# Routing's subtractions, products and constants from VectorE to GpSimd, with new offsets for the planner

## The chip, the cores and the metric

The kernel runs on one core of a Trainium2 chip. Its engines are TensorE (PE; PEld is its weight load), VectorE (DVE), ScalarE (ACT), GpSimd (POOL) and SyncE (SP, which here issues most of the DMAs). The metric is the time of one execution on the device, in microseconds (us), as the median of some runs. Engine times and the granted TensorE clock come from the profile of one execution.

## The reference

Attention in which each query keeps its 32 largest scores, then a mixture of eight experts, each token going to one expert or, by a skip gate, to none. Cut to what matters:

```python
B, H, S, D = 8, 8, 576, 64
scores = scale * np.matmul(q, k.transpose(0, 1, 3, 2))
kth = np.partition(scores, -32, axis=-1)[..., -32:-31]
scores = np.where(scores >= kth, scores, -1e9)
attn = softmax(scores)                      # with 1e-9 in the denominator
x = (attn @ v) as (B*S, H*D)                # N = 4608 tokens, DM = 512
do_compute = x @ w_skip > 0
e_idx = argmax(x @ w_gate, axis=1)          # E = 8 experts
gate_w = softmax(x @ w_gate)[e_idx]         # with 1e-9 in the denominator
out = x + do_compute * gate_w * (relu(x @ w1[e_idx]) @ w2[e_idx])   # F = 1024
```

## The kernel before

**Attention** takes the first 880 us or so. There are 32 pairs of heads, and each pair has nine rows of 128 queries: 288 rows in all. For one row:

- PE multiplies queries with keys into PSUM (L652).
- DVE takes the eight largest of each of seven chunks (L662, MAX8) and sorts out the row's list of candidates with MAX8 and MATCH_REPLACE8 (L668, L670).
- ACT copies the scores to SBUF as xc (L704) and makes a row of signs, r, with Sign (L684): which scores lie above the 24th largest.
- POOL multiplies the two into xw, called the push (L707), and DVE adds nine more columns (L716).
- DVE takes the eight largest of xw, the window (L728). The last of these is the 32nd largest score.
- ACT makes the penalty from it (L725, PEN): 0 for the scores that are kept.
- PE then makes the transposed scores with the penalty added (L867 to L874), ACT their exponential PT (L899), and PE the products with the values. DVE divides by the sums (L998, L1007), and prepares the gate's logits (L1012), which POOL adds up (L1022).

**Routing.** When the logits of a group of batches are there, `route()` (L370) finds each token's expert, its gate weight and its place in the expert's list. There are three groups: batches 0 to 3 (group 0, 20 tokens a partition, so 160 columns where it works over the experts), batches 4 to 6 (group 1, 15 and 120), and batch 7 (`end`). Its steps form one chain through `later()`: maximum, difference and comparison (L410 to L416), Exp on ACT, the gate weights (L432 to L434), a prefix sum on PE, rank and place from it (L437 to L450), and then a list for each batch (`lists()`, L469 to L487, in part on POOL already). Groups 0 and 1 are routed while the rows of later pairs go on, group 2 after attention.

**What sets the order.** A planner (`class Plan`, L176) takes every instruction as a task with engine, duration, predecessors and a due time, and picks for each engine, step by step, among the tasks that could start. Due times are the row's number plus the offsets in `K` and `FINE`; `LOOK`, `GAIN`, `KEEP` and `TURN` are the rules by which a later but more urgent task is preferred. The engines execute in the order that it writes out. A task that is given another engine, duration or offset thus changes the order of all that follows. `lock` is an amount that `route()` adds to the planned duration of some DVE instructions. The planner is run a second time for the start of the first expert, and with it goes routing of group 2.

**The experts** follow from about 880 us in a fixed order. `part_hi` (L1109, ACT) and `part_lo` (L1112, DVE) split each weight block into a high part and the remainder, the low part. The gathered tokens xg are transposed on PE (L1152) and split by ACT (xh, L1156) and DVE (xl, L1160); the first layer uses xh and xl with the weights' hi and lo parts (L1216 to L1218).

## Time and profile before

| | us |
|---|---|
| median of 3 runs | 1180.88 |
| lowest and highest | 1179.74, 1182.52 |
| the profiled execution | 1182.15 |
| its span, first to last instruction | 1180.3 |
| PE busy in it | 1117.7 (95%) |
| DVE busy | 1000.2 (85%) |
| ACT busy | 931.8 (79%) |
| POOL busy | 752.6 (64%) |
| mean granted TensorE clock | 0.981 of full speed |

The shares are averages over stages with different limits, attention up to some 880 us and the experts behind it, so they don't tell what bounds a stage. The rows below look at stretches, at single lines, and at who waited for whom.

### The profile page before, as it was taken

The numbers are of one execution on the slowest core, as the hardware profiler recorded it, in microseconds if no ns is written. First come the engines' busy times: TensorE is split into PE (matmuls) and PEld (weight loads), VectorE is DVE, ScalarE is ACT, GpSimd is POOL, SyncE is SP. The second block draws the span as 40 slices with busy tenths as digits, with TensorE's granted clock in tenths as the row PEclk, the third lists the DMA queues.
The fourth block names the chain that finished last, engine by engine and source line by source line (L and its number), as shares of the span: only waits on it lengthen the run. The fifth ranks groups of instructions, "written<-read, shape, count | busy, mean of one in ns | idle before, by whom it ended". The sixth has DMA issues, their size and how long they took to land. (4 is left out here: it accounts for less than half of the span.)

```text
span 1180.3 us, 37612 instructions
## 1 busy us (share of the span) xinstructions
PE 1117.7 (95%) x13012; PEld 947.0 (80%) x13012; DVE 1000.2 (85%) x5250; ACT 931.8 (79%) x1965; POOL 752.6 (64%) x997
## 2 busy tenths in 40 slices
PE   4899999999999999999999999999889999999996
PEld 3778888888888888788877878877778988888885
DVE  8999999999999999999999999999954756655531
ACT  5999999999999999999998999999862533333320
POOL 7778888777888877788875999777772112222210
PEclk8799999999999999999998999999999999999998
DMA  5545555644556554455544454443065654454300
GB/s 122 123 113 122 134 129 131 159 115 113 124 135 145 139 134 113 115 129 137 141 121 120 105 131 124 123 115 83 22 191 181 197 164 149 152 162 156 116 19 25
DMA packets 197404, 148.42 MB, mean 126 GB/s; under 512 B 100898, under 2 KB 162850, under 8 KB 197204
## 3 DMA queue, kind: packets, MB, share of 16 engines
q1 hardware_dynamic: 190340, 135.54, 44.8%
q0 software_dynamic: 3840, 9.47, 2.5%
q8 instruction: 105, 1.72, 0.6%
q10 hardware_dynamic: 3024, 0.90, 0.3%
q14 instruction: 95, 0.78, 0.2%
HBM read 68.31 MB, written 25.31 MB: 79 GB/s over the span
## 5 line engine op out<-in xcount | busy, mean ns | idle before, releaser
L707 POOL TENSOR_TENSOR xw<-xc,r 128x576 f32<-128x576 f32 x288 | 370.3, 1286 | 148.8 <-ACT r L684 143.4
L662 DVE MAX8 cand<-r 128x8 f32<-128x82 f32 (+1 forms) x2016 | 366.7, 234 | 3.0 <-PE r L652 2.9
L684 ACT ACTIVATE r<-xc,cl 128x576 bf16<-128x576 f32 x288 | 224.8, 780 | 16.3 <-DVE cl L668 15.3
L725 ACT ACTIVATE PEN<-xc,wn 128x576 bf16<-128x576 f32 x288 | 224.5, 780 | 3.7 <-DVE wn L728 3.6
L728 DVE MAX8 wn<-xw 128x8 f32<-128x585 f32 x288 | 217.2, 754 | 2.4 <-POOL xw L707 2.2
L867 PE MATMUL r<-QH,KK 128*128 128x256 f32 (+1 forms) x640 | 190.3, 324 | 10.1 <-ACT PT L899 4.5
L704 ACT ACTIVATE xc<-r 128x576 f32<-128x576 f32 x288 | 188.6, 655 | 9.5 <-DVE cand L662 3.9
L652 PE MATMUL r<-KK,QH 128*128 128x288 f32 x640 | 162.2, 344 | 14.0 <-ACT xc L704 6.6
L869 PE MATMUL r<-QL,KK 66*128 66x256 f32 (+1 forms) x640 | 174.5, 300 | 0.0
L668 DVE MAX8 cl<-cand 128x8 f32<-128x28 f32 (+2 forms) x864 | 166.7, 193 | 4.4
L899 ACT ACTIVATE PT<-r 128x576 f32<-128x576 f32 x256 | 166.9, 654 | 3.1 <-PE r L874 2.9
L1146 POOL DMA_INDIRECT out_dram<-ot,idx x24 | 24.5, 1022 | 213.8 <-DVE ot L1145 167.2
L1112 DVE TENSOR_TENSOR lo<-raw,hi 128x1024 fp32r<-128x1024 f32 x64 | 79.2, 1241 | 72.0 <-ACT hi L1109 71.1
L652 PE MATMUL r<-KK,QL 66*128 66x288 f32 x640 | 135.1, 302 | 0.0
L867 PEld LDWEIGHTS r<-QH,KK 128*128 128x128 f32 x640 | 119.0, 192 | 17.5 <-ACT PT L899 7.4
L874 PE MATMUL r<-nbi,PEN 128*128 128x128 bf16 (+1 forms) x1632 | 132.8, 217 | 0.0
L652 PEld LDWEIGHTS r<-KK,QH 128*128 128x128 f32 x640 | 98.2, 196 | 41.0 <-ACT PT L899 12.2
L1109 ACT ACTIVATE hi<-raw 128x1024 fp32r<-128x1024 f32 x64 | 67.2, 1055 | 71.6 <-PE py L1241 71.4
L869 PEld LDWEIGHTS r<-QL,KK 66*128 66x128 f32 x640 | 119.9, 193 | 0.3 <-issue 0.2
L652 PEld LDWEIGHTS r<-KK,QL 66*128 66x128 f32 x640 | 103.9, 194 | 0.3 <-issue 0.3
L1221 ACT ACTIVATE hh<-ph 128x352 fp32r<-128x352 f32 (+2 forms) x72 | 31.1, 433 | 92.5 <-PE ph L1218 89.4
L670 DVE MATCH_REPLACE8 cand<-cl,cand 128x28 f32<-128x28 f32 x576 | 103.3, 179 | 0.0
(256 smaller groups left out, 2575.4 us busy)
## 6 DMA issues: line engine op xcount, KB each, us to landing
raw<-in_moe_w_dram SPq DMA_DIRECT2D x64, 512.0 KB
...
QH<-HI SPq DMA_DIRECT2D x124, 144.0 KB
...
```

What stands on the lines that cost most here:

```text
L652: nc.tensor.matmul(R(u, w), t[0:k0, c:c + P], KH[i2][0:k0, HB * hd + u:HB * hd + w], start=(k0 == P and x == 0), stop=(k0 < P and x == len ...
L662: nc.vector.max(C[s][:, c], R(CH[c], CH[c + 1]))
L668: nc.vector.max(L[:, 4 * r:4 * r + 8], c)
L684: nc.scalar.activation(RR[s], XC[s], AF.Sign, bias=CL[p][:, i, 23:24], scale=-ODD, accum_out=CN[:, s:s + 1])
L704: nc.scalar.activation(XC[s], R(), AF.Copy)
L707: nc.gpsimd.tensor_tensor(xw()[:, 0:S], XC[s], RR[s], op=OP.mult)
L725: nc.scalar.activation(pen, XC[s], AF.Relu, bias=least, scale=-1.0)
L728: nc.vector.max(WN[p][:, i], XW[s] if out_ else R())
L867: nc.tensor.matmul(t, KH[i2][:, ks], QH[i2][:, qs], start=(y == 0), stop=False)
L869: nc.tensor.matmul(t, KO[i2][:, ks], QL[i2][0:D + 2, qs], start=False, stop=False)
L874: nc.tensor.matmul(rb[:, O + c:O + c + z - a], PEN[p][:, PS * i + REM + c0 - o:PS * i + REM + c0 - o + P], nbi[:, a:z], start=False, stop= ...
L899: return pl.add("ACT", 0.535, due + K["ex"] + FINE["ex"][at], lambda: nc.scalar.activation(dst, st["r"], AF.Exp, scale=scale), x, give=[h])
```

## The change

For groups 0 and 1, eleven of routing's DVE instructions are issued on GpSimd: the difference to the maximum, the products, the constants, the split of a place into low and high, and the last sums. L413 and L415, of two operations each, become two instructions each, in every group: thirteen GpSimd instructions a group. Reductions, casts, the comparison that makes the one-hot and the three-operand forms stay on DVE. With `end`, all stays on DVE, with the two more instructions. `lock` goes from 0.25 to 0.7, and to 0 for `end`.

The first expert's four low parts go from DVE to GpSimd, planned at 2.4 us each.

Three predecessors differ. A penalty doesn't wait for the row before any more. Sign waits for the push of three rows ago (`PUSHD`) instead of that row's penalty. The pair's penalty buffer, which is now named when a row is set up, is waited for by each of its rows. `SG` is empty, so what depends on it changes nothing. All offsets and rules of the planner have new values, so that the order differs on every engine, at the start as well.

```diff
-LOOK, GAIN, KEEP = 0.164, 7.176, 67.94
-DRAIN, TURN = 0.2, 39.21
+LOOK, GAIN, KEEP = 0.064, 7.612, 66.883
+DRAIN, TURN = 0.2, 43.29
...
-        lock = 0.25
-        def later(f, dur, *after):
-            x = pl.add("DVE", dur, st["due"], f, u, after)
+        lock = 0.0 if end else 0.7
+        G_ = V_ if end else nc.gpsimd
+        def later(f, dur, *after, pool=None):
+            x = pl.add("DVE", dur, st["due"], f, u, after) if end or not pool else \
+                pl.add("POOL", 0.19 + 0.0022 * pool, st["due"], f, u, after)
...
-        later(lambda: V_.tensor_sub(T["d"], l8, bc(T["mx"])), wide + lock)
-        vx = later(lambda: V_.scalar_tensor_tensor(T["val"], T["d"], 0.0, wb, op0=OP.is_equal, op1=OP.mult), wide + lock)
+        later(lambda: G_.tensor_tensor(T["d"], l8, bc(T["mx"]), op=OP.subtract), wide, pool=n * E)
+        later(lambda: G_.tensor_scalar(T["val"], T["d"], 0.0, None, op0=OP.is_equal), wide, pool=n * E)
+        vx = later(lambda: G_.tensor_tensor(T["val"], T["val"], wb, op=OP.mult), wide, pool=n * E)
         later(lambda: V_.tensor_reduce(mb, T["val"], axis=AX, op=OP.max), wide)
-        later(lambda: V_.scalar_tensor_tensor(mb, lb[:, :, E], 0.0, mb, op0=OP.is_gt, op1=OP.mult), small + lock)
+        later(lambda: G_.tensor_scalar(T["col"], lb[:, :, E], 0.0, None, op0=OP.is_gt), small, pool=n)
+        later(lambda: G_.tensor_tensor(mb, T["col"], mb, op=OP.mult), small, pool=n)
...
-        later(lambda: V_.tensor_scalar(T["gt"], T["gt"], 1e-9, None, op0=OP.add), small + lock)
+        later(lambda: G_.tensor_scalar(T["gt"], T["gt"], 1e-9, None, op0=OP.add), small, pool=n)
...
-        later(lambda: V_.tensor_add(T["val"], T["sr"][:, 0:n], base[:, b0:b0 + 1].to_broadcast([P, n, E])), wide + lock, srx)
-        later(lambda: V_.tensor_mul(T["val"], T["val"], T["oh"]), wide + lock)
+        later(lambda: G_.tensor_tensor(T["val"], T["sr"][:, 0:n], base[:, b0:b0 + 1].to_broadcast([P, n, E]), op=OP.add), wide, srx, pool=n * E)
+        later(lambda: G_.tensor_tensor(T["val"], T["val"], T["oh"], op=OP.mult), wide, pool=n * E)
...
-        later(lambda: V_.tensor_copy(lo, T["ri"]), small)
-        later(lambda: V_.tensor_sub(hi, T["rk"], lo), small + lock)
+        later(lambda: G_.tensor_copy(lo, T["ri"]), small, pool=n)
+        later(lambda: G_.tensor_tensor(hi, T["rk"], lo, op=OP.subtract), small, pool=n)
...
-        later(lambda: V_.tensor_scalar(T["col"], mb, -float(NB), float(EB + 1), op0=OP.mult, op1=OP.add), small)
+        later(lambda: G_.tensor_scalar(T["col"], mb, -float(NB), float(EB + 1), op0=OP.mult, op1=OP.add), small, pool=n)
...
-        rx = later(lambda: V_.tensor_scalar(T["col"], T["col"], 1.0, None, op0=OP.subtract), small)
-        bx = pl.add("DVE", 0.07, st["due"], lambda: V_.tensor_add(base[:, b0 + nb], base[:, b0], T["sr"][:, n]), rx)
+        rx = later(lambda: G_.tensor_scalar(T["col"], T["col"], 1.0, None, op0=OP.subtract), small, pool=n)
+        bx = later(lambda: G_.tensor_tensor(base[:, b0 + nb], base[:, b0], T["sr"][:, n], op=OP.add), small, pool=E)
...
-            rr = A("ACT", 0.765, s + D_["kt"] + J("kt"), above_out, x, tx, PENNED.get(s - 3), lag=-0.06)
+            rr = A("ACT", 0.629 if i in SG else 0.765, s + D_["kt"] + J("kt"), above_out, x, None if i in SG else tx, PUSHD.get(s - 3), give=[h] if i in SG else (), lag=-0.06)
...
-            x = [A("POOL", 1.31, s + D_["push"] + J("push"), push_out, rr, OUTW[-2:-1]), fx]
+            PUSHD[s] = A("POOL", 1.31, s + D_["push"] + J("push"), push_out, rr, tx, OUTW[-2:-1])
+            x = [PUSHD[s], fx]
...
-            kx = PENNED[s] = A("POOL" if i in PP else "ACT", 1.56 if i in PP else 0.672, s + D_["rf"] + J("rf"), below_out, x, PENNED.get(s - 1), TU.get(p - 2) if i == 0 else None)
+            kx = PENNED[s] = A("POOL" if i in PP else "ACT", 1.56 if i in PP else 0.672, s + D_["rf"] + J("rf"), below_out, x, TU.get(p - 2))
...
-    def part_lo(w, i):
-        nc.vector.tensor_sub(WLO[w][i], WRAW[w][i], WHI[w][i])
+    def part_lo(w, i, eng=nc.vector):
+        eng.tensor_tensor(WLO[w][i], WRAW[w][i], WHI[w][i], op=OP.subtract)
...
-        PARTED.append(pl.add("DVE", 1.13, D0 + 1 + i, lambda i=i: part_lo(0, i), x))
+        PARTED.append(pl.add("POOL", 2.4, D0 + 1 + i, lambda i=i: part_lo(0, i, nc.gpsimd), x))
```

The lines after are numbered anew: L707 (push) becomes L714, L728 (window) L733, L684 (Sign) L691, L437 L443, L1112 L1118, L1156 L1162. The reductions, casts and comparisons of routing that stay on DVE and read what POOL has made are L419, L422, L440, L445, L451, L453 and L475 there.

The first place is the second half of group 0's routing, on DVE, between the windows and lists of the rows; `rsr` is the prefix sum, `rval` its masked value, `rmx` the rank. Before:

```order
L728 MAX wn_12042<-xw_12643 128x8 [waits Pool_49]
L668 MAX cl_12597<-cand_12636 128x8 [waits DVE_49]
L437 TENSOR_TENSOR rval_9695<-rsr_9697,base_165 128x160
L670 MATCH_REPLACE cand_12636<-cl_12597,cand_12636 128x7x4 [waits DVE_49]
L438 TENSOR_TENSOR rval_9695<-rval_9695,roh_9696 128x160 [waits DVE_49]
L668 MAX cl_12597<-cand_12636 128x8 [waits DVE_49]
L716 TENSOR_SCALAR xw_12721<-wo_103,CN_106 128x9 [waits Activation_49]
L670 MATCH_REPLACE cand_12636<-cl_12597,cand_12636 128x7x6 [waits DVE_49]
L439 TENSOR_REDUCE rmx_9691<-rval_9695 128x20
L668 MAX cl_12597<-cand_12636 128x8 [waits DVE_49]
L440 CAST rri_9698<-rmx_9691 128x20 [waits DVE_49]
```

After, on DVE:

```order
L733 MAX wn_12040<-xw_12415 128x8 [waits Pool_49]
L675 MAX cl_12039<-cand_12455 128x8 [waits DVE_49]
L445 TENSOR_REDUCE rmx_9676<-rval_9680 128x20 [waits Pool_49]
L677 MATCH_REPLACE cand_12455<-cl_12039,cand_12455 128x7x4 [waits DVE_49]
L723 TENSOR_SCALAR xw_12516<-wo_103,CN_106 128x9 [waits Activation_49]
L675 MAX cl_12039<-cand_12455 128x8 [waits DVE_49]
L733 MAX wn_12040<-xw_12484 128x8 [waits Pool_49]
L677 MATCH_REPLACE cand_12455<-cl_12039,cand_12455 128x7x6 [waits DVE_49]
L446 CAST rri_9683<-rmx_9676 128x20
L675 MAX cl_12039<-cand_12455 128x8 [waits DVE_49]
```

And after, on POOL:

```order
L714 TENSOR_TENSOR xw_12415<-xc_12352,r_12393 128x576 [waits Activation_49]
L443 TENSOR_TENSOR rval_9680<-rsr_9682,base_165 128x160 [waits Activation_49]
L444 TENSOR_TENSOR rval_9680<-rval_9680,roh_9681 128x160 [waits Pool_49]
L714 TENSOR_TENSOR xw_12484<-xc_12420,r_12465 128x576 [waits Activation_49]
L714 TENSOR_TENSOR xw_12516<-xc_12481,r_12495 128x576 [waits DVE_49,Activation_49]
L933 TENSOR_TENSOR sum_12554<-PT1_124 128x576 [waits Activation_49]
L448 CAST rank_167<-rri_9683 128x20 [waits DVE_49]
L449 TENSOR_TENSOR rank_167<-rmx_9676,rank_167 128x20 [waits Pool_49]
L714 TENSOR_TENSOR xw_12586<-xc_12533,r_12567 128x576 [waits Activation_49]
```

The addition (L437, now L443) and the product (L438, now L444) have left DVE and stand between two pushes on POOL; the reduction on DVE (now L445) waits for POOL, and so do what follows it on POOL for DVE.

The second place is the start of the first expert, the four low parts of its first weights (`lo00` to `lo03`). Before, on DVE, behind the index of the gather and one division by the sums:

```order
L1131 TENSOR_TENSOR idx0_202<-ti24_17887,LS_169 128x24 [waits DVE_49]
L998 RECIPROCAL sm_17922<-pt_17904 128x4 [waits PE_49]
L1007 TENSOR_TENSOR xb_17637<-pt_17904,sm_17922 128x2x2x64 [waits DVE_49]
L1012 TENSOR_TENSOR lgt_17925<-pt_17904,sm_17922 128x36
L1112 TENSOR_TENSOR lo00_17802<-raw00_17794,hi00_17798 128x1024 [waits DMAHW3_49,DMAHW5_49,DMAHW2_49,DMAHW6_49,DMAHW1_49,DMAHW7_49,DMAHW0_49,Activation_49]
L1112 TENSOR_TENSOR lo01_17803<-raw01_17795,hi01_17799 128x1024 [waits DMAHW2_49,Activation_49]
L1112 TENSOR_TENSOR lo02_17804<-raw02_17796,hi02_17800 128x1024 [waits DMAHW4_49,DMAHW6_49,DMAHW3_49,Activation_49]
L1112 TENSOR_TENSOR lo03_17805<-raw03_17797,hi03_17801 128x1024 [waits DMAHW4_49,Activation_49]
L998 RECIPROCAL sm_18039<-r2_148 128x4 [waits PE_49]
```

After, on POOL, behind the logits' additions:

```order
L1028 TENSOR_TENSOR lg_150<-lg_150,lgt_17908 128x2x2x9 [waits DVE_49]
L1028 TENSOR_TENSOR lg_150<-lg_150,lgt_17872 64x9
L1028 TENSOR_TENSOR lg_150<-lg_150,lgt_17872 64x9 [waits Pool_49]
L933 TENSOR_TENSOR sum_17930<-PT0_123 128x576 [waits Activation_49]
L1118 TENSOR_TENSOR lo00_17831<-raw00_17823,hi00_17827 128x1024 [waits DMAHW3_49,DMAHW6_49,DMAHW2_49,DMAHW7_49,DMAHW1_49,Activation_49]
L1118 TENSOR_TENSOR lo01_17832<-raw01_17824,hi01_17828 128x1024 [waits DMAHW2_49,Activation_49]
L1118 TENSOR_TENSOR lo02_17833<-raw02_17825,hi02_17829 128x1024 [waits DMAHW3_49,DMAHW4_49,DMAHW0_49,Activation_49]
L1118 TENSOR_TENSOR lo03_17834<-raw03_17826,hi03_17830 128x1024 [waits DMAHW4_49,Activation_49]
L1234 MEMSET hh0_18108 128x32 [waits PE_49]
```

The four subtractions moved from a stretch of DVE between two divisions to POOL, between a sum of PT and the zeroing of the hidden layer's buffers.

The third place is ACT at the same point of the program: `xh` are the split tokens of the first expert, the DMAs are the stores of batch 7. Before:

```order
L1156 ACTIVATE xh0_17807<-pa_18052 128x4x128 [waits PE_49,Pool_49]
L366 DMA xd_193<-xb_18042 512x1x128 [waits DVE_49]
L367 DMA xd_193<-xb_18042 64x128 [waits DVE_49]
L366 DMA out_0_dram<-xb_18042 512x1x128
L367 DMA out_0_dram<-xb_18042 64x128
L1156 ACTIVATE xh0_17807<-pt_18061 128x4x128 [waits PE_49]
```

After:

```order
L1162 ACTIVATE xh0_17836<-pt_17978 128x4x128 [waits PE_49,Pool_49]
L982 ACTIVATE os0_144<-r2_148 128x256 [waits PE_49,Activation_49]
L984 ACTIVATE os0_144<-r2_148 128x128 [waits Activation_49]
L982 ACTIVATE os1_145<-r0_146 128x64 [waits PE_49,Activation_49]
L984 ACTIVATE os1_145<-r0_146 128x64
L1162 ACTIVATE xh0_17836<-pa_18063 128x4x128 [waits PE_49]
L367 DMA xd_193<-xb_17986 512x1x128 [waits DVE_49]
L368 DMA xd_193<-xb_17986 64x128 [waits DVE_49]
L367 DMA out_0_dram<-xb_17986 512x1x128
L368 DMA out_0_dram<-xb_17986 64x128
```

The second `xh` instruction stood behind the four stores and stands ahead of them now; the first stands ahead of attention's last outputs (`os`).

Over the rows 36 to 215, the number of ACT instructions between a row's Sign and its penalty is 10.5 on the mean before and 9.4 after; seven or fewer stand between them in 2 rows before and in 17 after.

## Rows read from the trace of the kernel before

**Rows 1.** Busy time by stretch, all engines; columns named in the first line.

```profile
core 0: us, PE busy (x) PEld busy (x) DVE busy (x) ACT busy (x) POOL busy (x), PEclk, DMA share, GB/s
100.00:600.00 500.00, 496.18 (x6915) 415.29 (x6915) 493.19 (x2987) 494.59 (x1091) 395.81 (x508) 1.00 0.54 130
460.00:500.00 40.00, 39.63 (x522) 33.00 (x522) 39.63 (x238) 39.02 (x86) 29.09 (x37) 1.00 0.52 126
600.00:850.00 250.00, 235.64 (x3203) 193.93 (x3204) 244.16 (x1411) 229.40 (x499) 197.23 (x265) 0.98 0.44 106
860.00:880.00 20.00, 19.30 (x412) 16.42 (x405) 9.66 (x21) 11.93 (x25) 16.32 (x25) 1.00 0.69 196
```

**Rows 2.** ACT's waits, 600 to 850 us: total us, times, longest us.

```profile
ACT r L684 <- DVE cl L668: 13.0, 18, 2.0
ACT PEN L725 <- DVE wn L728: 3.1, 4, 1.8
ACT xc L704 <- DVE cand L662: 2.6, 5, 0.7
```

**Rows 3.** Routing on DVE, 440 to 850 us: ns min/median/max, first and last start.

```profile
L412 DVE TENSOR_TENSOR rd<-lg,rmx x2: 273/300/326, 468.7 to 787.3; 128x160 f32<-128x160 f32 x1, 128x120 f32<-128x120 f32 x1
L413 DVE SCALAR_TENSOR_TENSOR rval<-rd,wts x2: 267/286/304, 471.5 to 787.7; 128x160 f32<-128x160 f32 x1, 128x120 f32<-128x120 f32 x1
L415 DVE SCALAR_TENSOR_TENSOR m<-lg,m x2: 506/864/1222, 475.1 to 788.9; 128x20 f32<-128x20 f32 x1, 128x15 f32<-128x15 f32 x1
L433 DVE TENSOR_SCALAR rgt<-rgt x2: 154/370/585, 495.4 to 791.4; 128x20 f32<-128x20 f32 x1, 128x15 f32<-128x15 f32 x1
L437 DVE TENSOR_TENSOR rval<-rsr,base x2: 283/954/1625, 609.1 to 793.4; 128x160 f32<-128x160 f32 x1, 128x120 f32<-128x120 f32 x1
L438 DVE TENSOR_TENSOR rval<-rval,roh x2: 253/748/1242, 610.8 to 793.9; 128x160 f32<-128x160 f32 x1, 128x120 f32<-128x120 f32 x1
L442 DVE CAST rank<-rri x2: 1168/1276/1384, 618.5 to 800.0; 128x20 f32<-128x20 int32 x1, 128x15 f32<-128x15 int32 x1
L443 DVE TENSOR_TENSOR rank<-rmx,rank x2: 153/168/183, 619.7 to 803.8; 128x20 f32<-128x20 f32 x1, 128x15 f32<-128x15 f32 x1
L446 DVE TENSOR_SCALAR rcol<-m x2: 977/1038/1098, 628.2 to 821.5; 128x20 f32<-128x20 f32 x1, 128x15 f32<-128x15 f32 x1
L449 DVE TENSOR_SCALAR rcol<-rcol x2: 640/872/1103, 637.5 to 837.3; 128x20 f32<-128x20 f32 x1, 128x15 f32<-128x15 f32 x1
L450 DVE TENSOR_TENSOR base<-base,rsr x2: 446/938/1429, 638.7 to 840.4; 128x8 f32<-128x8 f32 x2
```

**Rows 4.** DVE in order of time, group 1: start us, us, instruction.

```profile
788.86 1.22 DVE L415 SCALAR_TENSOR_TENSOR m<-lg,m 128x15 f32<-128x15 f32 x1
790.01 0.24 DVE L662 MAX8 cand<-r 128x8 f32<-128x82 f32 x1
```

**Rows 5.** The windows of all rows on DVE: ns min/median/max.

```profile
L728 DVE MAX8 wn<-xw x288: 741/753/774, 23.2 to 861.7; 128x8 f32<-128x585 f32 x144
```

**Rows 6.** POOL's groups by line and shape: busy us, mean ns, idle before.

```profile
L707 POOL TENSOR_TENSOR xw<-xc,r 128x576 f32<-128x576 f32 x288 | 370.3, 1286 | 148.8 <-ACT r L684 143.4 <-DMA QH<-HI 2.0 <-DVE wn L728 0.2
L565 POOL TENSOR_TENSOR LO<-TT,HI 128x640 fp32r<-128x640 f32 x62 | 96.9, 1562 | 0.0
...
L747 POOL COPY FL<-cl 128x9 f32<-128x9 f32 x32 | 6.3, 198 | 0.0
...
L474 POOL TENSOR_TENSOR rrh<-rrh,tabs 128x120 bf16<-128x120 bf16 x14 | 5.3, 387 | 0.7 <-DVE rrh L469 0.7
```

**Rows 7.** DVE in order of time, the first expert's low parts.

```profile
872.16 1.28 DVE L1112 TENSOR_TENSOR lo<-raw,hi 128x1024 fp32r<-128x1024 f32 x1 [0.22 <-ACT hi L1109]
873.66 4.49 DVE L1112 TENSOR_TENSOR lo<-raw,hi 128x1024 fp32r<-128x1024 f32 x3 [0.21 <-ACT hi L1109]
```

**Rows 8.** ACT and PE in order of time, the first expert's start.

```profile
880.81 0.60 ACT L1156 ACTIVATE xh<-pa 128x512 fp32r<-128x512 f32 x1 [1.33 <-POOL hl L1228]
...
883.61 0.60 ACT L1156 ACTIVATE xh<-pt 128x512 fp32r<-128x512 f32 x1 [2.20 <-issue]
...
884.26 0.37 PE L1216 MATMUL ph<-xh,hi 128*128 128x224 f32 x1 [3.11 <-ACT xh L1156]
```

More of the change, by code (lines that the diff above doesn't have):

```diff
@@ L30 @@
         ("PE", "PE"): 0.0}
-LOOK, GAIN, KEEP = 0.164, 7.176, 67.94
-DRAIN, TURN = 0.2, 39.21
-K = dict(qk=-6.436, cand=-7.822, kt=-6.355, push=-12.756, count=2.92, window=2.675, kth=4.11, rf=40.955, pen=-24.387, u0=6.301, u1=10.019, av=-0.812, a0=2.517, a1=7.268, a2=2.062, co=45.04, sm=-27.744, ca=48.91, tx=-2.41, rt=9.211, rd=-4.985, rs=1.779, pp=12.011, ps=0.546, mx=16.505, f3=5.424, f4=2.403, f5=-9.516, ex=-28.018, us=-0.294, cs=-44.193, ch=0.074, ce=-10.653, lg=3.943, ld=11.234, hl=6.901, hs=-0.757, moe=22.067)
@@ new lines @@
+LOOK, GAIN, KEEP = 0.064, 7.612, 66.883
+DRAIN, TURN = 0.2, 43.29
+K = dict(qk=-6.619, cand=-9.062, kt=-7.285, push=-11.437, count=0.262, window=2.329, kth=1.605, rf=44.311, pen=-29.958, u0=5.294, u1=10.014, av=-0.829, a0=1.79, a1=8.997, a2=2.612, co=44.959, sm=-39.182, ca=53.074, tx=1.762, rt=6.307, rd=-5.024, rs=1.518, pp=11.655, ps=0.751, mx=15.599, f3=5.603, f4=5.279, f5=-10.627, ex=-26.731, us=-0.264, cs=-39.106, ch=-1.491, ce=-13.139, lg=4.38, ld=10.168, hl=5.169, hs=-0.931, moe=30.767)
+FINE = dict(qk=(0.844, -6.14, 2.287, -9.743, 2.969, -3.805, -11.381, -2.256, 1.703), ch=(-1.084, 1.956, -0.532, 1.345, -0.377, 0.45, 0.638, 1.632, -0.47), cand=(2.79, 4.82, -0.677, 7.317, -4.95, 8.155, -18.969, 9.59, -4.974), tx=(-11.584, 9.144, 14.265, 6.386, 3.692, 3.598, 3.025, 3.344, -6.332), kt=(8.833, -12.74, 15.792, 4.984, -16.613, 8.945, 4.41, 7.43, -12.313), push=(5.551, -5.689, -8.402, -6.967, -7.333, -11.07, -19.358, -2.801, -22.505), fill=(-1.421, -13.358, -3.786, 9.834, -9.573, 10.556, 4.377, -4.823, -14.417), window=(-1.642, 5.785, 0.632, -0.261, 4.502, -0.929, 2.34, -0.327, -5.628), rf=(-22.877, 17.515, 3.875, -7.315, 11.627, -25.11, 18.355, 4.14, -13.049), u=(2.27, -1.207, 3.423, 0.11, -0.402, -0.372, 2.078, 1.216, -0.372), ex=(1.255, 8.484, -19.601, -6.095, -2.278, -8.464, 1.705, 5.398, 13.519), f1=(0.957, -7.893, 7.012, -7.51, 3.954, 0.776, -18.07, -1.522, -4.449, 0.179, 7.242, -8.771, -7.181, -3.851, 3.356), f2=(-4.29, -7.542, 3.596, -6.206, 0.121, -3.931, -0.095, -33.138, -5.109), f3=(1.119, -11.677, 0.472, 1.182, -8.423, -6.705), f4=(2.011, -3.532, -1.841), f5=(-3.458, 14.286, 14.192, 7.345, 11.239, -4.44, 3.283, -2.391, -0.385), pp=(0.086, 0.946, 0.244), pa=(-3.367, -0.745, 3.911), hl=(3.165, -0.735, 3.144, 0.867), mx=(0.338, 3.47, 7.323, 2.331, -26.165, -7.784), sm=(-0.55, -8.842, 17.735, 2.101, -5.444, 7.721))
@@ L40 @@
 PP = ()
+SG = ()
 SA = 1
@@ L635, in row @@
         i2 = p % NQ
+        PEN[p] = PEN_[p % 2]
         out_ = i in OUT
-        h = Hold(RW, 1 if out_ else 2)
+        h = Hold(RW, 1 if out_ and i not in SG else 2)
         R = lambda u=0, w=S: h.t[:, LO_ + u:LO_ + w]
@@ L683, in above_out @@
             RR[s] = wk.tile([P, S], BF, name="r", bufs=3)
-            nc.scalar.activation(RR[s], XC[s], AF.Sign, bias=CL[p][:, i, 23:24], scale=-ODD, accum_out=CN[:, s:s + 1])
+            nc.scalar.activation(RR[s], R() if i in SG else XC[s], AF.Sign, bias=CL[p][:, i, 23:24], scale=-ODD, accum_out=CN[:, s:s + 1])
         def count():
@@ L718, in below_out @@
         def below_out():
-            if i == 0:
-                PEN[p] = PEN_[p % 2]
             pen, least = PEN[p][:, PS * i + REM:PS * (i + 1)], WN[p][:, i, 7:8]
@@ L793, in row @@
             FLAGGED[p] = A("POOL", 0.47, s + 3, flags, kx, WINS[p])
-    RF, XC, XW, OUTB, OUTW, WINS = {}, {}, {}, [], [], {}
+    RF, XC, XW, OUTB, OUTW, WINS, PUSHD = {}, {}, {}, [], [], {}, {}
     PS = S + REM
```

1 line of the change is left out of this document (removed).

## The prediction

> **What bounds the kernel now.** I read the windows first, then the waits, then the lines that the diff names. From 100 to 600 us three engines are full at once: TensorE (PE) is busy 496.18 of 500 us, VectorE (DVE) 493.19, ScalarE (ACT) 494.59 [rows 1]. A change there pays only if it relieves all three. From 600 to 850 us, still inside attention, that balance is gone: DVE is busy 244.16 of 250 us, ACT only 229.40, PE 235.64 [rows 1]. Measured by the idle share of the steady stretch (DVE 6.81 of 500, ACT 5.41, PE 3.82), DVE stands idle 5.84 − 3.4 = 2.4 us more than usual, ACT 20.6 − 2.7 = 17.9, PE 14.36 − 1.9 = 12.5. The waits name the cause: ACT waits there for DVE's lists (L668) 13.0 us, for DVE's window (L728) 3.1 and for its candidates (L662) 2.6, in all 18.7 us [rows 2], which is ACT's excess. So DVE sets the pace from 600 to 850 us, and what leaves DVE there shortens the run by up to 12.5 us; then PE, and at 17.9 us ACT, is full again. What DVE does there beyond the rows' own work is the routing of two groups of batches: the second half of group 0 (609 to 640 us) and all of group 1 (787 to 841 us) [rows 3].
>
> **What leaves DVE.** The eleven moved lines, both groups, are [rows 3]; with two instances each, minimum plus maximum is their sum: L412 0.60, L413 0.57, L415 1.73, L433 0.74, L437 1.91, L438 1.50, L442 2.55, L443 0.34, L446 2.08, L449 1.74, L450 1.88 us; together 15.6 us for 22 instructions. DVE starts the next instruction before one has ended: L415 of group 1 begins at 788.86 and lasts 1.22 us, and the next begins at 790.01, 0.07 before its end [rows 4]. So some 0.08 us of each is no slot, and 22 × 0.08 = 1.8 us come off: 13.8 us of slots. Four of them, L412, L413, L415 and L433 of group 0, lie at 468 to 496 us, where the first starts are [rows 3]. The long L415 is group 1's [rows 4], so that group 0's has 0.51 us; with the longer instance of the other three it is at most 0.33 + 0.30 + 0.51 + 0.58 = 1.72 us, 1.4 without the overlap. The other 12.4 us lie between 600 and 850 us. At 460 to 500 us ACT idles only 0.98 us of 40, 0.55 above its steady share [rows 1], so of the 1.4 only **0.5 us** can shorten anything. Of the 12.4 I take off DVE's own excess idle of 2.4, time in which DVE was not the last: **10.0 us**, under PE's 12.5.
>
> **Why these instructions are long, and whether that stays.** The same line takes 0.28 and 1.63 us (L437), 0.15 and 0.58 (L433), 0.45 and 1.43 (L450) [rows 3]; the long ones are longer by about one push on GpSimd (POOL), 1.29 us [rows 6]. The 128x585 maximum of L728 took 741 to 774 ns in all 288 cases [rows 5], though POOL was busy 79% of 600 to 850 us [rows 1]. So certain DVE operations wait for a POOL instruction to end and the maxima, which are most of DVE's work, don't. A page of the Trainium skill speaks against the change here: "Perfetto Trace Analysis", section "Optimizing Scalar/DVE Operations", says that GpSimd and VectorE share a read port of SBUF, so that offloading between the two might not help. The stretched L437 agrees with a shared port, the even L728 does not agree with the conclusion; by the rule as it stands the 10.0 us would come back as longer DVE instructions, which is rival B. By the rows, an instruction that has left DVE can no longer be stretched there, and I count the full slot.
>
> **What POOL takes up.** Thirteen instructions a group. No row shows them on POOL; the nearest are a multiply of 128x120 at 0.39 us, a copy of 128x9 at 0.20 and the push of 128x576 at 1.29 [rows 6]. Five of a group's thirteen are wide. Group 1's have 120 columns, group 0's 160, for which the slope from 120 to 576 columns gives 0.47 us: 5 × 0.47 + 8 × 0.2 = 3.95 us and 5 × 0.39 + 8 × 0.2 = 3.55, together 7.5 us. POOL has 250 − 197.23 = 52.8 us idle from 600 to 850 us [rows 1], and over the run it waits 143.4 us ahead of pushes for ACT's Sign [rows 6]; that covers them. A push that comes behind one of them is late by 0.2 to 0.47 us. Without that cover the price is the 7.5 us themselves.
>
> **The new waits.** The chain now changes engine: on DVE the reductions, casts and comparisons L419, L422, L440, L445, L451, L453 and L475 of the new numbering wait for POOL, seven a group. Behind them on DVE stand the maxima of the next rows, and for these wait ACT's Sign and penalty. Lower bound 0: the planner has set other work in between, as at L445, where one window and one list lie between the multiply's place and the reduction. Upper bound: each waits for one push, 14 × 1.29 = 18 us. Such waits on POOL are rare now, so I take one in ten: **+2.0 us**.
>
> **The low parts.** Four subtractions of 128x1024 leave DVE, 1.28 us for the first and 4.49 for the other three at 872 to 878 us [rows 7]. DVE is busy 9.66 of 20 us there [rows 1]: gain 0, the idle time covers them. On POOL one costs, by 1.56 us for 128x640 [rows 6], about 1.56 × 1024/640 = 2.5 us, four 10 us. If the first begins at 872.2 as now, the last ends at 882.2 at the earliest; with the additions that the order sets ahead of them, some 3 us later. The first expert's matmuls begin at 884.26 and the first that needs a low part comes at once behind [rows 8]. Speaking for a gain there: ACT's second xh began at 883.61, 2.2 us late behind four store issues [rows 8], which the new order sets behind it. A gain of up to those 2.2 us against a loss of up to 3 us if the fourth low part is late: I take **0**, because the low parts end just where they are wanted. Routing of the last batch keeps DVE and gains two instructions, 0.3 us in all by the short L412; the experts behind it are full of PE work: 0.
>
> **Order.** Penalties no longer wait for the row before, Sign waits for the push of three rows ago instead of that row's penalty, and every offset is new. In 100 to 600 us ACT has 5.41 us idle [rows 1], so freer penalties give 0 to 5.4 us; on the other side stands rival C. I take 0.
>
> **Sum.** 10.0 + 0.5 − 2.0 = 8.5 us off the profiled execution's 1182.15: 1173.65. That execution lies 1.27 us above the median of 1180.88, so the forecast is 1172.4 us.
>
> **Rivals.** *B, the freed time half comes back* as waits of DVE for POOL's answers, or by the port. For: fourteen new handovers, each behind a push of 1.29 us. Against: L728's evenness and POOL's idle time. Half of 10.0: 1177.4 us. *C, the new order starves ACT in the steady part, slower than before.* Between a row's Sign and its penalty, both on ACT, its push (1.29 us [rows 6]) and its window (0.75 [rows 5]) must pass: 2.04 us, and twice that where each stands behind another of its kind, as happens on a POOL that is 79% and a DVE that is 99% busy [rows 1]. Other ACT instructions have to fill that; one takes 494.59/1091 = 0.45 us [rows 1], so seven cover 3.2. In the two orders, over rows 36 to 215, the penalty has at most seven ACT instructions between itself and its Sign in 2 of 180 rows before and in 17 of 180 after. Over 288 rows that is 24 more rows; at 3.1/4 = 0.78 us for such a wait [rows 2] 18.7 us: 1191 us. It decides from 11 such waits on (8.5/0.78), the others being hidden. Against: the mean is still 9.4 instructions (10.5 before), and a late penalty lets others pass now. *D, the slots on DVE are not the limit*: PE, whose 12.5 us of excess idle could be another dependency's, keeps the pace, and nothing changes: 1181. Against: the 18.7 us of ACT's waits name DVE. *E, the steady part gains as well*, the whole 5.4 us: 1167, and with the transition's 2.2 us 1165.
>
> **How the numbers follow.** Forecast 0.60, between 1166 and 1177; B 0.13; C 0.14; D 0.08; E 0.05. A measurement of this kernel can tell 0.2%, 2.4 us, from no change: faster is below 1178.5, slower above 1183.2. Forecast, B (but for 0.01) and E are faster: 0.77; D and a weak C (0.02) with that 0.01 give 0.10 the same; C otherwise, and a bad D, slower: 0.13. The range is to leave out two tenths: below, E with the transition and with waits at their bound of 0, 1163; above, D whole and the beginning of C, 1182.
>
> **What would show it.** Right: DVE's busy time down by 13 us or so, ACT's waits for L668's successor between 600 and 850 us cut from 13.0 to below 6 us, attention's end (the first xh at 880.81 us [rows 8]) 8 us earlier, 100 to 600 us as full as before, and the expert phase of the same length. B would show as DVE waits on POOL for the reductions and casts of routing, above 6 us in sum, or as longer maxima. C would show as ACT's share from 100 to 600 us down by 2% or more, with waits of the penalty for the window. The forecast is wrong if the stretch up to 600 us changes by more than 5 us, or if PE restarts in the first expert more than 3 us later behind the last low part.

## The result: 1167.54 us, and the profile after

The changed kernel takes 1167.54 us (median of 4 runs, 1166.89 to 1168.53) against 1180.93 for the kernel before in the same comparison: 13.4 us less, a ratio of 0.9886 with a 95% interval of 0.9869 to 0.9904. The forecast was 1172.4, and the range reached from 1163 to 1182. The profiled execution took 1168.11 us, its span is 1166.2.

The busy time by stretch, with the columns of [rows 1], shows the stretch that was forecast to change:

```profile
100.00:600.00 500.00, 498.26 (x6975) 415.28 (x6967) 491.98 (x2990) 494.97 (x1095) 399.55 (x515) 1.00 0.54 131
...
600.00:850.00 250.00, 245.35 (x3443) 203.08 (x3447) 242.13 (x1474) 242.30 (x531) 218.90 (x308) 1.00 0.44 106
```

From 100 to 600 us the engines are as full as before (ACT busy 494.97 us against 494.59), though the windows there come later, as the table below shows. From 600 to 850 us ACT is busy 242.30 us instead of 229.40 and PE 245.35 instead of 235.64; DVE does 1474 instructions in less busy time than 1411 took before. ACT's waits there, which were 18.7 us [rows 2]:

```profile
ACT r L691 <- DVE cl L675: 2.3, 8, 0.4
ACT xc L711 <- DVE cand L669: 1.4, 4, 0.5
ACT PEN L730 <- DVE wn L733: 1.0, 3, 0.4
```

The Sign's waits for the lists fell from 13.0 us to 2.3. Routing's steps on POOL, of which [rows 3] had the DVE forms (ns min/median/max, first and last start):

```profile
L416 POOL TENSOR_TENSOR rd<-lg,rmx x2: 385/423/461, 473.8 to 781.0; 128x160 f32<-128x160 f32 x1, 128x120 f32<-128x120 f32 x1
L417 POOL TENSOR_SCALAR rval<-rd x2: 519/576/634, 475.6 to 781.8; 128x160 f32<-128x160 f32 x1, 128x120 f32<-128x120 f32 x1
L443 POOL TENSOR_TENSOR rval<-rsr,base x2: 435/480/525, 601.1 to 790.5; 128x160 f32<-128x160 f32 x1, 128x120 f32<-128x120 f32 x1
L448 POOL CAST rank<-rri x2: 195/197/199, 608.1 to 794.1; 128x20 f32<-128x20 int32 x1, 128x15 f32<-128x15 int32 x1
```

Their spread is gone: L437 took 0.28 and 1.63 us on DVE, L443 takes 0.44 and 0.53 on POOL; the 26 steps take 8.6 us. The windows on DVE, the four low parts on POOL, and the pushes (against [rows 5] and [rows 6]):

```profile
L733 DVE MAX8 wn<-xw x288: 710/752/772, 24.0 to 850.6; 128x8 f32<-128x585 f32 x144
```

```profile
L1118 POOL TENSOR_TENSOR lo<-raw,hi 128x1024 fp32r<-128x1024 f32 x4 | 9.3, 2361 | 0.0
L714 POOL TENSOR_TENSOR xw<-xc,r 128x576 f32<-128x576 f32 x288 | 369.9, 1286 | 125.9 <-ACT r L691 114.9 <-DVE cand L677 3.3 <-DVE cl L675 1.8
```

And the start of the first expert, ACT and then PE in order of time, against [rows 8]:

```profile
863.86 0.62 ACT L1162 ACTIVATE xh<-pt 128x512 fp32r<-128x512 f32 x1
...
868.06 0.60 ACT L1162 ACTIVATE xh<-pa 128x512 fp32r<-128x512 f32 x1 [1.23 <-PE pa L1158]
868.06 0.63 ACTq L367 DMA_DIRECT2D xd<-xb  x1
```

```profile
868.71 0.37 PE L1222 MATMUL ph<-xh,hi 128*128 128x224 f32 x1 [0.69 <-ACT xh L1162]
```

The last window starts 11.1 us earlier (850.6 against 861.7), the first expert's first matmul 15.6 us earlier (868.71 against 884.26), the end 14.1 us.

**Where the time went.** The 288 windows, numbered from 0 in order of time, are a ruler that all kernels share. The table gives the us between the starts of windows, from the start of the span to window 153, between windows, and from the last to the end of the span; the kernels of the experiments below stand beside. Windows 153 to 198 hold the first part of group 0's routing, 198 to 225 its second part (in the changed kernel with all four of its lists, before with two), 261 to 279 most of group 1's.

| kernel | to 153 | 153–198 | 198–225 | 225–261 | 261–279 | 279–287 | to the end | span |
|---|---|---|---|---|---|---|---|---|
| before | 457.7 | 129.2 | 86.7 | 104.8 | 57.9 | 25.5 | 318.6 | 1180.3 |
| changed | 464.4 | 127.1 | 78.5 | 104.2 | 54.8 | 21.6 | 315.6 | 1166.2 |
| e1_engine_alone | 457.1 | 129.8 | 82.9 | 104.8 | 56.5 | 25.3 | 319.5 | 1176.0 |
| e2_engine_back | 462.4 | 129.3 | 79.7 | 104.2 | 56.7 | 21.6 | 315.9 | 1169.8 |
| e5_old_offsets | 465.3 | 130.6 | 81.9 | 119.3 | 55.3 | 23.5 | 323.4 | 1199.3 |
| e6_offsets_alone | 465.9 | 130.1 | 81.9 | 107.6 | 59.3 | 23.1 | 315.3 | 1183.2 |
| e9_pad_vector | 456.8 | 132.2 | 87.8 | 104.8 | 60.8 | 27.4 | 319.3 | 1189.2 |
| e10_old_rules | 468.0 | 127.8 | 78.5 | 105.4 | 54.4 | 23.4 | 317.5 | 1175.1 |
| e13_replanned | 456.3 | 129.4 | 81.1 | 111.9 | 53.8 | 23.7 | 324.2 | 1180.4 |

So the changed kernel loses 6.7 us before window 153, gains 2.1 + 8.2 + 3.1 = 13.4 in the three stretches with routing, 0.6 between them, 3.9 in attention's last eight rows and 3.0 from the last window to the end. That the three stretches give 13.4 us and the medians 13.4 too is chance: the other terms nearly cancel. The first and the last column scatter most. Kernels below that share the changed order (e2_engine_back, e3_low_back, e12_pad_gpsimd) have 462.4 to 463.2 up to window 153, and 315.9 to 316.8 at the end.

**TensorE's clock in the second part of group 0.** A part of the 8.2 us is the clock. Two pieces of that stretch in the kernel before and the whole of it (columns of [rows 1]), then the same windows in the changed kernel and in e1_engine_alone:

```profile
615.90:619.30 3.40, 3.40 (x46) 3.03 (x35) 3.40 (x17) 3.38 (x9) 3.40 (x6) 0.50 0.50 116
...
643.20:650.00 6.80, 6.39 (x77) 5.81 (x78) 6.70 (x37) 5.92 (x13) 4.46 (x4) 0.50 0.78 180
...
586.90:673.60 86.70, 81.30 (x1090) 68.47 (x1089) 84.64 (x477) 78.22 (x171) 65.46 (x87) 0.94 0.47 112
```

```profile
591.50:670.00 78.50, 77.62 (x1090) 64.03 (x1090) 76.29 (x472) 76.29 (x168) 69.36 (x102) 1.00 0.52 125
```

```profile
586.90:669.80 82.90, 77.94 (x1090) 64.69 (x1089) 78.34 (x469) 78.11 (x171) 67.47 (x94) 1.00 0.49 118
```

PE does 1090 matmuls in each. In the kernel before 10.2 us of the stretch ran at the lower of the clock's two levels (0.50, 1.2 GHz), and the matmuls took 81.30 us instead of 77.62. So 3.7 of the 8.2 us are the clock, and 4.5 are PE's idle time, which fell from 5.4 to 0.9 us. In e1_engine_alone 3.4 of its 3.8 us are the clock. At both places PE had to wait for ACT, 1.7 us until 614.3 and 2.2 us until 643.6 (total us, times, longest us):

```profile
PE r L652 <- ACT xc L704: 2.2, 1, 2.2
PE r L867 <- ACT PT L899: 1.7, 1, 1.7
```

The longest wait of PE in this stretch is 0.3 us in the changed kernel and 1.2 in e1_engine_alone. It fits that shorter waits kept the clock up, but no run tests that by itself.

### The profile page after: what moved, and what is told of

Read it like the earlier page. It is cut to its first block, busy times and chain, and to the rows that moved or that the text cites. A ratio compares the mean times of both kernels' runs of the same rounds, so it can differ in the third digit from the quotient of the medians.

```text
span 1166.2 us, 37790 instructions
## 1 busy us (share of the span) xinstructions
PE 1109.4 (95%) x13012; PEld 939.3 (81%) x13012; DVE 977.8 (84%) x5226; ACT 929.9 (80%) x1965; POOL 763.6 (65%) x1027
## 5 line engine op out<-in xcount | busy, mean ns | idle before, releaser
L714 POOL TENSOR_TENSOR xw<-xc,r 128x576 f32<-128x576 f32 x288 | 369.9, 1286 | 125.9 <-ACT r L691 114.9
L669 DVE MAX8 cand<-r 128x8 f32<-128x82 f32 (+1 forms) x2016 | 384.6, 233 | 6.2 <-PE r L659 5.5
L691 ACT ACTIVATE r<-xc,cl 128x576 bf16<-128x576 f32 x288 | 222.9, 774 | 6.8 <-DVE cl L675 4.4
L730 ACT ACTIVATE PEN<-xc,wn 128x576 bf16<-128x576 f32 x288 | 220.8, 771 | 3.1 <-DVE wn L733 2.9
L733 DVE MAX8 wn<-xw 128x8 f32<-128x585 f32 x288 | 216.3, 752 | 3.5 <-POOL xw L714 3.2
L711 ACT ACTIVATE xc<-r 128x576 f32<-128x576 f32 x288 | 184.0, 640 | 6.7 <-DVE cand L669 4.5
L675 DVE MAX8 cl<-cand 128x8 f32<-128x28 f32 (+2 forms) x864 | 164.3, 191 | 5.0
L905 ACT ACTIVATE PT<-r 128x576 f32<-128x576 f32 x256 | 162.0, 641 | 2.1 <-PE r L880 2.1
L1118 DVE TENSOR_TENSOR lo<-raw,hi 128x1024 fp32r<-128x1024 f32 x60 | 73.6, 1227 | 72.2 <-ACT hi L1115 71.2
L873 PEld LDWEIGHTS r<-QH,KK 128*128 128x128 f32 x640 | 118.7, 191 | 15.6 <-ACT xc L711 5.4
L956 PE MATMUL pa<-PT,V 128*32 128x256 f32 (+1 forms) x2144 | 102.9, 323 | 0.2 <-ACT PT L905 0.2
```

The source lines that it names most:

```text
L669: nc.vector.max(C[s][:, c], R(CH[c], CH[c + 1]))
L675: nc.vector.max(L[:, 4 * r:4 * r + 8], c)
L691: nc.scalar.activation(RR[s], R() if i in SG else XC[s], AF.Sign, bias=CL[p][:, i, 23:24], scale=-ODD, accum_out=CN[:, s:s + 1])
L711: nc.scalar.activation(XC[s], R(), AF.Copy)
L714: nc.gpsimd.tensor_tensor(xw()[:, 0:S], XC[s], RR[s], op=OP.mult)
L730: nc.scalar.activation(pen, XC[s], AF.Relu, bias=least, scale=-1.0)
```

## Experiments: engine and order taken apart

The change puts routing on another engine and writes a new order. Since the engines execute in the order written, the two can be separated: the same order, with the steps issued on the other engine at the same places.

**The engine alone, in the old order.**

```diff
 # before.py, planned as before
-        later(lambda: V_.tensor_sub(T["d"], l8, bc(T["mx"])), wide + lock)
+        later(lambda: G_.tensor_tensor(T["d"], l8, bc(T["mx"]), op=OP.subtract), wide + lock)
...
```

> The kernel before with its own offsets, order and dependencies; only routing's eleven steps of groups 0 and 1 are issued on GpSimd, each at the place in the program where the DVE instruction stood (the two-operation steps as two instructions). Theory (DVE sets the pace from 600 to 850 us, and the moved instructions are its excess): 10.5 us come off DVE's slots, less some handovers that nobody planned for: 1180.9 - 10.5 + 2 to 5 = 1172 to 1176 us, attention's last window 6 us or more earlier. Rival (the gain is the new order's, or comes back in waits of DVE for GpSimd): above 1178 us, with waits of DVE for POOL above 6 us in sum.

Measured: 1178.02 us against 1181.62, a ratio of 0.9975 (0.9965 to 0.9985), 3.6 us less. The time is just at the rival's bound, and its sign is nearly there: 5.8 us of waits of DVE for POOL, where it named 6. DVE's waits from 440 to 850 us (total us, times, longest):

```profile
...
DVE roh L423 <- POOL m L421: 1.2, 1, 1.2
DVE m L418 <- POOL rval L416: 1.2, 1, 1.2
DVE rrh L476 <- POOL rcol L456: 1.0, 1, 1.0
DVE rcol L454 <- POOL rcol L453: 0.9, 1, 0.9
DVE rmx L446 <- POOL rval L445: 0.9, 1, 0.9
DVE gt L441 <- POOL rgt L440: 0.6, 1, 0.6
...
```

The kernel before has none of these. POOL, too, waits for its turn in the chain, and the pushes behind wait with it:

```profile
...
POOL rval L444 <- ACT rsr L437: 2.4, 1, 2.4
POOL rd L413 <- DVE cl L675: 2.0, 1, 2.0
...
```

DVE's time in routing's steps fell by 14.5 us (table below), and the run gained 3.6.

**The new order alone, with the steps on DVE.**

```diff
 # after.py
-        G_ = V_ if end else nc.gpsimd
+        G_ = V_
```

> The changed kernel with its own order on every other engine; only routing's steps of groups 0 and 1 are issued on DVE again, at the places where the GpSimd instructions stood. Theory: they are long again beside pushes (about 1 us each for half of them), 10 to 14 us more: 1178 to 1182 us. Rival (the order carries the gain): within 4 us of 1167.5.

Measured: 1172.06 us, ratio 0.9922 (0.9905 to 0.9938). The theory, by which the engine carries the gain, falls: with routing back on DVE two thirds of it are still there. Of 13.4 us, 4.5 need the engine, in this order; 3.6 came from it in the old one. 9.6 us come with the order, and 3.6 + 9.6 makes 13.2. "The order" here is all that the change brings besides the engine: the offsets and rules, the predecessors, `lock` (no run changes that alone) and the place of each step.

Why does the order matter that much, with the same steps on the same engine? DVE's summed durations of all of routing's steps (moved or not) by place, in us:

| | 440–560 us | 590–720 us | 770–860 us |
|---|---|---|---|
| before | 3.78 | 13.70 | 12.00 |
| e2_engine_back | 4.39 | 6.63 | 10.29 |
| e1_engine_alone | 2.08 | 6.11 | 6.78 |
| changed | 1.85 | 4.11 | 5.85 |
| e9_pad_vector | 6.36 | 16.25 | 16.44 |

In the second part of group 0 the new order halves DVE's time without any other engine, 7.1 us less, and the stretch of windows 198 to 225 is 7.0 us shorter (3.2 us of that is the same matmuls at the higher granted clock); around group 1 DVE has 1.7 us less, and the stretch 1.2. Before, in order of time on POOL and on DVE:

```profile
608.95 1.55 POOL L565 TENSOR_TENSOR LO<-TT,HI 128x640 fp32r<-128x640 f32 x1
610.47 1.36 POOL L707 TENSOR_TENSOR xw<-xc,r 128x576 f32<-128x576 f32 x1
```

```profile
609.06 1.62 DVE L437 TENSOR_TENSOR rval<-rsr,base 128x160 f32<-128x160 f32 x1
...
610.77 1.24 DVE L438 TENSOR_TENSOR rval<-rval,roh 128x160 f32<-128x160 f32 x1
```

L437 begins 0.11 us after POOL's instruction and ends 0.18 us after its end (610.68 against 610.50); L438 ends 0.18 us after the push. In e2_engine_back the same two steps on DVE, and POOL:

```profile
600.15 1.28 POOL L714 TENSOR_TENSOR xw<-xc,r 128x576 f32<-128x576 f32 x1 [1.10 <-ACT r L691]
603.46 1.28 POOL L714 TENSOR_TENSOR xw<-xc,r 128x576 f32<-128x576 f32 x1 [2.02 <-ACT r L691]
```

```profile
601.39 0.32 DVE L443 TENSOR_TENSOR rval<-rsr,base 128x160 f32<-128x160 f32 x1
...
602.35 0.31 DVE L444 TENSOR_TENSOR rval<-rval,roh 128x160 f32<-128x160 f32 x1
```

They fall into a gap between two pushes, and take 0.32 and 0.31 us. One reason is at hand: the planner had put these steps on POOL, so it had reserved POOL's time for them, whichever engine then does them. It is not the whole reason. In e2_engine_back 6 of the 26 steps still take 0.75 to 0.94 us beside a POOL instruction (13 of 22 took 0.45 to 1.63 us before). And e6_offsets_alone below, planned with routing on DVE, has its seven moved steps of this part at 3.9 us in all, against 7.7 before and 2.7 in e2_engine_back. So some of it is how the steps happen to fall in a new order.

Of the 22 moved instructions of the kernel before, 14 begin while a POOL instruction runs, and all 14 end 0.03 to 0.18 us after that instruction's end; the other 8 take 0.15 to 0.33 us. The Trainium skill, "SBUF — State Buffer", section "SBUF: two separate sides", says that DVE with two SBUF inputs or in a two-port mode and GpSimd exclude each other for a whole instruction; the 14 ends agree with that, and the MAX8 of [rows 5], with one input, agrees as well.

**Is DVE's time the currency?** More of it, nothing moved:

```diff
 # before.py; each of ten moved steps of groups 0 and 1
+                f()
+                for _ in range(2):
+                    V_.tensor_reduce(T["pad"], l8, axis=AX, op=OP.max)
```

> The kernel before in its own order, with 40 reductions of the logits (128x160 and 128x120, into a scratch tile that nobody reads) added on VectorE, two behind each of ten of routing's moved steps, groups 0 and 1; about 0.2 us of a slot each, 8 us in all. Theory of the prediction (VectorE's time is the currency there): 1189 us. Rival (a few handovers set the time, not VectorE's sum, so that only part counts): 1182 to 1185 us.

Measured: 1190.32 us against 1180.5, 9.8 us more. Routing's time on DVE grew by 9.6 us (29.48 to 39.05 in the table: 11.7 us for the 40 reductions, and 2.2 less for the other steps), and the stretches with routing by 3.0, 1.1 and 2.9, the last eight rows by 1.9. Adding on DVE costs about one to one. Taking away did not pay one to one in e1_engine_alone; the new waits above are a part of the reason, and the rest isn't traced.

**POOL's cover.**

```diff
 # after.py, behind each POOL step of groups 0 and 1
+                    if pool > n:
+                        nc.gpsimd.tensor_tensor(T["padw"], l8, l8, op=OP.subtract)
...
```

> The changed kernel in its own order; each of routing's GpSimd steps of groups 0 and 1 is followed by a subtraction of the same size into a scratch tile that nobody reads: 26 instructions, some 7.5 us of GpSimd time. Theory of the prediction (GpSimd's idle time covers them): within 2 us of 1167.5. Rival (a push comes late behind each, and DVE and ACT wait for pushes): 1171 to 1175 us.

Measured: 1168.52 us, ratio 0.9884 (0.9868 to 0.9901), the ratio of the changed kernel to within 0.0002. POOL's time in routing goes from 8.6 to 16.4 us and doesn't show in the kernel's time.

**Offsets, predecessors, planning.** Each of the next four was planned anew, so its order differs everywhere.

```diff
-LOOK, GAIN, KEEP = 0.064, 7.612, 66.883
-DRAIN, TURN = 0.2, 43.29
+LOOK, GAIN, KEEP = 0.164, 7.176, 67.94
+DRAIN, TURN = 0.2, 39.21
...
```

This is the changed kernel with the old numbers, K and FINE included:

> The changed kernel with the planner's old offsets and rules (K, FINE, LOOK, GAIN, KEEP, TURN of before). Theory (the engine move carries the gain): 1168 to 1173 us, without the start's loss of 4.5 us that the changed kernel shows by its 36th to 198th windows. Rival (the new offsets carry it): above 1176 us.

And the reverse, the kernel before with the new numbers:

> The kernel before with the planner's new offsets and rules, all else as before. Theory: routing still on DVE, so no gain from 600 to 850 us, and the start's loss of some 4.5 us: 1181 to 1187 us. Rival (offsets carry the gain): below 1174 us.

Measured: 1202.35 us (1.018; 1.0163 to 1.0197) and 1186.29 us (1.0042; 1.0028 to 1.0056). The changed code with the old offsets is 21 us slower than before, the old code with the new ones 5 us slower. Neither half gains without the other. In e5_old_offsets two routing stretches are short (81.9 and 55.3), but windows 225 to 261 take 119.3 us instead of 104.8 (10.2 us of it at the lower granted clock), and the end 323.4. Some of this is routing itself, moved: group 0's chain ends behind window 230, and all four lists come after it. In e6_offsets_alone windows 198 to 225 take 81.9 us with routing on DVE and all four lists in them, 4.8 less than before: a new order can shorten this stretch without the engine.

```diff
 # e10_old_rules: after.py
-above_out, x, None if i in SG else tx, PUSHD.get(s - 3), ...
+above_out, x, None if i in SG else tx, PENNED.get(s - 3), ...
-below_out, x, TU.get(p - 2))
+below_out, x, PENNED.get(s - 1), TU.get(p - 2) if i == 0 else None)
```

> The changed kernel with the three old predecessors (a penalty waits for the row before's, Sign for the penalty of three rows ago, the push for Sign alone), planned anew with the new offsets. If the freer predecessors carry part of the gain: 1172 us or more. If they only come along: within 3 us of 1167.5.

Measured: 1176.57 us (0.9949; 0.9933 to 0.9966), 9 us slower than the changed kernel by the medians and 7 by the ratios. So the freer predecessors carry a part of the gain, as far as offsets that came together with them can tell. The routing stretches stay (78.5 and 54.4); the loss lies before window 153 (3.6 us), in windows 225 to 261 (1.2), and at the end of attention and behind it (1.8 + 1.9).

```diff
 # e13_replanned: before.py with routing planned and issued on GpSimd, lock 0.7
+        G_ = V_ if end else nc.gpsimd
+                pl.add("POOL", 0.19 + 0.0022 * pool, st["due"], f, u, after)
```

> The kernel before with routing's steps planned and issued on GpSimd as in the changed kernel (lock 0.7), but with the old offsets, the old predecessors and the low parts on VectorE. Theory (planning the steps on GpSimd puts them into its gaps, so that the waits of e1_engine_alone are met): 1170 to 1175 us. Rival (old offsets fit only the old tasks, a new plan disturbs far more): above 1178 us.

Measured: 1183.18 us (1.0017; 1.0006 to 1.0028). The rival's time, but not the rival's story alone: windows 198 to 225 gain 5.6 us and 261 to 279 4.1, and the new plan loses them in windows 225 to 261 (7.1 us) and from the last window to the end (5.6 us). The first gain is in part routing that has moved: group 0's chain ends behind window 229 and all four lists come after 233, so that they fall into the stretch that loses. Still DVE's time in routing from 590 to 720 us is 6.8 us, against 13.7 before. The loss at the end is mostly the first expert's start: its first matmul comes 27.7 us behind the last window (27.9 in e5_old_offsets, 22.6 before). So both plans with the old offsets take time from DVE, and lose as much or more elsewhere. How much of windows 225 to 261 is the moved routing, and what the rest is, I haven't settled.

**Start, transition, low parts.**

```diff
 # e8_stores_behind: before.py, the last batch's store is planned behind the split of the tokens
+    XBFREE[NP - 1] = store(b, lambda: XB[NP - 1], ..., due, DONE[NP - 1] + [XT], True)
```

> The kernel before; only the four store issues of the last batch on ACT stand behind the second split of the first expert's tokens (xh) instead of ahead of it. Theory (this is the transition's gain, 2 to 3 us between the last window and the end, which the changed kernel, its version with routing back on VectorE, and the offsets alone all show): 1178.5 us, PE's first matmul of the expert 2.2 us earlier. Rival (the stores come later and the last batch's gather waits for them): 1181 us.

Measured: 1180.08 us against 1180.5, ratio 0.9988 (0.9979 to 0.9997): 0.4 us less by the medians, 1.4 by the ratio, whose interval reaches from 0.4 to 2.5 us and so doesn't exclude 2.2. PE's first matmul came 20.3 us behind the last window instead of 22.6, but the next tokens' split 42.8 instead of 44.0, and the end 317.3 instead of 318.6: half of what the start won is lost again before the second set of tokens. In the changed kernel and in those with its order there the first matmul comes 18.1 to 18.3 us behind the last window; but their ends lie at 315.6 to 317.3, so that the transition gains 1.3 to 3.0 us. The stores' 1.3 can be all of that or less than half. Of the kernels planned anew e6_offsets_alone has it, too (315.3), and e13_replanned and e5_old_offsets, with old offsets, haven't (324.2, 323.4): there it goes with the new offsets.

```diff
 # e3_low_back: after.py
-... lambda i=i: part_lo(0, i, nc.gpsimd), x))
+... lambda i=i: part_lo(0, i), x))
```

> The changed kernel with its own order; only the first expert's four low parts are issued on VectorE, where they were before. Theory (VectorE idles there, and a low part is wanted only by the pair of hidden blocks whose weights it holds, so GpSimd's 2.36 us each are hidden as well): within 1.5 us of 1167.5. Rival (9.4 us of GpSimd time behind attention hold up the gathers and routing of the last batch): 2 to 4 us faster than the changed kernel.

Measured: 1169.08 us, ratio 0.9903 (0.9888 to 0.9918), which overlaps the changed kernel's. The low parts' engine makes no difference that shows. In the changed kernel they run on POOL, and end before the first matmul that reads one begins (POOL, then PE, in order of time):

```profile
860.23 9.34 POOL L1118 TENSOR_TENSOR lo<-raw,hi 128x1024 fp32r<-128x1024 f32 x4
```

```profile
870.76 0.27 PE L1224 MATMUL ph<-xh,lo 128*128 128x224 f32 x1
```

```diff
 # e4_start_old: after.py
+    K.update(EARLY_K)
+    FINE.update(EARLY_FINE)
     for p in range(NP):
+        if p == 2:
+            K.update(LATE["K"])
+            FINE.update(LATE["FINE"])
```

> The changed kernel with the planner's old K and FINE for the first two pairs of heads and the new ones from the third pair on. Theory (the start of the changed kernel is 4.5 us late by its 36th to 198th windows, and with three full engines that is never caught up): 1163 us. Rival (the first rows only look late, or the seam costs as much): 1167 us or more.

Measured: 1165.3 us (1164.41 to 1166.88), ratio 0.9864 (0.9849 to 0.9879). That is 2.2 us below the changed kernel's 1167.54 in the medians; the runs of the two don't overlap, but by 0.01 us only, and the intervals of the ratios do. So a gain isn't shown, though this median is the lowest here. Window 153 starts at 461.1 us instead of 462.4 to 464.4 in the kernels with the changed start: 1.3 to 3.3 us of the late start are got back.

```diff
 # e4_start_old, with the seam (where the new values set in) at another pair, and rules and predecessors of before ahead of it
-        if p == 2:
+        if p == SEAM:
...
+            LOOK, GAIN, KEEP, TURN = (0.164, 7.176, 67.94, 39.21) if at < SEAM * 25.6 else (0.064, 7.612, 66.883, 43.29)
...
-above_out, x, None if i in SG else tx, PUSHD.get(s - 3), ...
+above_out, x, None if i in SG else tx, PUSHD.get(s - 3) if p >= SEAM else PENNED.get(s - 3), ...
```

> The planner's old offsets, rules and predecessors for the first 16 pairs of heads, the changed kernel's from there on; routing on GpSimd as in the changed kernel. Theory (the changed kernel's rows 0 to 153 are 6.7 us later than before's, its gain lies behind them, and a seam costs little): 1160 to 1163 us. Rival (the seam costs what the start gives, or the later order depends on the earlier one): 1166 us or more.

Measured: 1171.28 us (0.9907; 0.9891 to 0.9924). Window 153 starts at 457.0, 7.4 us earlier than in the changed kernel, and more than that is lost behind the seam: windows 153 to 198 take 130.5 us instead of 127.1, 225 to 261 106.9 instead of 104.2, 261 to 279 57.2 instead of 54.8. The later offsets are good behind their own beginning only.

## Why the prediction was right in its time, and where its steps were wrong

**What bounds: right, but for the clock.** DVE sets the pace from 600 to 850 us. e9_pad_vector shows it (9.6 us more on DVE, 9.8 us more in all), and ACT's 18.7 us of waits fell to 4.7, as forecast. Rival D, by which nothing changes, falls with it. What the prediction gave no term is TensorE's clock: [rows 1] has it at 0.98 from 600 to 850 us, and PE's busy time there was taken for work. From window 198 to 225 the clock is 3.7 us of the gain.

**The sum for routing: right in its direction, too small, and wrong in its cause.** It forecast 10.5 us off and 2.0 back; the three routing stretches gained 13.4, the clock's 3.7 among them. The step "I count the full slot", by which each instruction that leaves DVE gives its slot, is not what happened. In the old order the same departure gave 3.6 us (e1_engine_alone), and with the instructions kept on DVE the new order gave 9.6 (e2_engine_back). The reason stood in the prediction's own paragraph: 14 of the 22 were long only because a POOL instruction ran beside them. Of their 15.6 us some 13.6 belong to those 14, which alone would take about 0.2 us each, so 10 us or so were waiting for POOL, and such waiting can be removed by a better place as well as by another engine.

**The new waits: 2.0 us was near neither end.** The changed kernel has no wait of routing on DVE for POOL that the view of waits shows, in the old order there are 5.8 us. How many there are goes with whether the order was planned with POOL's durations: the seven other kernels here that were planned so, with routing on POOL, show 0.6 us at most. Rival B named such waits; it forecast 1177.4 us, and e1_engine_alone took 1178.0. The Trainium skill, "Perfetto Trace Analysis", section "Optimizing Scalar/DVE Operations", by which offloading between the two might not help, comes near to that run, though what shows there is waits and not longer DVE instructions.

**What POOL takes up: right.** 8.6 us against 7.5 forecast, and e12_pad_gpsimd shows that they are covered.

**The low parts: the mechanism was misread, the term of 0 was too small.** That all four end just where they are wanted was wrong: a weight block serves two hidden blocks, so the fourth is wanted last. And they didn't begin at 872.2 us as before but at 860.2, so that all had ended by 869.6, ahead of the first matmul that reads one (870.76). No cost shows on either engine (e3_low_back). The stretch from the last window to the end, which the prediction put at 0 with at most 2.2 us of gain, gained 3.0, and 1.3 to 2.7 in the kernels of the same order.

**Order: the term of 0 was a difference of two larger ones.** The start lost 6.7 us up to window 153 (kernels that share this order lost 4.7 to 6.7), attention's last eight rows gained 3.9. No row of the trace before could give either. By the prediction's own sign of being wrong, a change of more than 5 us up to 600 us, this is its edge: 6.7 us later at window 153, 4.6 at window 198. The time came out at rival E's 1167 us by luck: E had the steady part gain, and it lost.

**Rival C: wrong indicator.** ACT's share from 100 to 600 us did not move. Seventeen rows with few ACT instructions between Sign and penalty gave no wait for the window there.
